# Quarter-width first V products, idle-time matmuls, and an earlier memory update in an attention and gMLP block

## The chip, the core and the metric

The kernel runs on one core of one Trainium2 chip. The core has five engines that each work through their own queue of instructions in order: TensorE (PE, with the loading of weights shown apart as PEld), VectorE (DVE), ScalarE (ACT), GpSimd (POOL) and SyncE (SP). In this kernel SP only issues transfers (DMA). The metric is the device time of one execution in microseconds (us), median of several runs. Before the change three runs took 826.48, 826.85 and 830.27 us.

## What is computed

A block of two parts on a sequence of 2048 tokens with 1024 channels, all in bf16. Part A is attention with a compressive memory: 32 heads of 32 channels, four segments of 512 tokens. Within a segment it is causal softmax attention; from one segment to the next a memory `M` (32 by 32 per head) and its normalizer `z` are carried. Part B is a gMLP. Both have a layer norm ahead and a residual.

```python
def _A_ref(x, wq, wk, wv, wo, beta):      # x is layernorm of the input
    q, k, v = heads(x @ wq), heads(x @ wk), heads(x @ wv)
    g = sigmoid(beta)
    M = 0; z = 0
    for s in range(4):
        qs, ks, vs = q[:, :, s], k[:, :, s], v[:, :, s]
        p = softmax(qs @ ks.T * scale + mask)
        a_dot = p @ vs
        pq = phi(qs)                      # t + 1 where t > 0, else exp(t)
        a_mem = (pq @ M) / (pq @ z + 1e-6)
        outs.append(g * a_mem + (1 - g) * a_dot)
        pk = phi(ks)
        M = M + pk.T @ vs
        z = z + sum(pk)
    return concat(outs) @ wo
def _B_ref(x, w_in, w_sp, b_sp, w_out):   # x is layernorm of h
    z = gelu(x @ w_in)
    z1, z2 = z[:, :1792], layernorm(z[:, 1792:])
    return (z1 * (w_sp @ z2 + b_sp)) @ w_out
h = x + A(layernorm(x)); out = h + B(layernorm(h))
```

## The kernel before

A small recorder collects the instructions of each engine in the order of the program text and puts a semaphore wait wherever one engine's instruction touches what another has written or read. So the order in the text is the order of every queue. Two rules matter here: for PSUM, the memory that TensorE writes to, the recorder counts whole banks of 512 fp32 columns, and any access to a bank by another engine has to be over before the next one begins; and all transfers are issued by SP, in order.

**Start.** SP issues the loads: x chunks 0 and 1 (`XCH`, 128 tokens each, 256 KB), the first 512 columns of `WV` (1 MB), x chunks 2 and 3, the first 256 columns of `WK` and of `WQ`, `beta`, and the rest of `WV`, `WK`, `WQ` and all of `WO` (9 MB in all). POOL and DVE build the identity matrix `IDENT`. For each of the four chunks of segment 0, DVE computes the layer norm statistics (`stats_of`), POOL the reciprocal root, DVE normalizes into `LNO` (`ln_apply`); TensorE transposes it in eight blocks and ACT evicts them to `XNT` (`pe_T`), and a V product follows (`proj_v`, eight matmuls accumulating over 1024 channels into one bank, evicted by ACT into `V`). Then `gates()` computes the gate `GS`, its complement `OMG` and the table `MASKG` (on DVE), with which the memory is masked by head; two products make K and Q of unit 0 (`proj_qk`), and `phi(0)` its feature maps.

**Units.** The loop from line 650 runs over 32 units n; unit n is segment s = n // 8 and a group c = n % 8 of four heads. In every unit TensorE does, in this order: logits of round 0; a filling f1 (K of the next unit); PV of round 2 of the unit before; logits of round 1; filling f2 (Q of the next unit); PV of round 0; logits of round 2 and, from segment 1 on, the product with the memory (`mem`); filling f3; PV of round 1; the memory update (`state`); filling f4 in segments 1 to 3. The logits go to banks 0 to 3, PV accumulates in banks 4 and 5, and everything else takes banks 6 and 7 in turn (`next_bank`). Fillings f3 and f4 are V products of 512 columns or output products (`wo`) of the segment before. Behind logits, ACT computes the exponentials (`E`) and POOL zeroes the masked triangle. `norm` (DVE) normalizes the output of a unit out of banks 4 and 5; the first PV of the next unit can start only after it. `mem_norm` (DVE: `rdm`, `tm`) does the same for the memory's part, behind ACT's third exponential.

`phi(n + 1)` is called behind f3: ACT's exp into `ETMP`, three DVE instructions, and SP's transposing transfer of the keys' features into `PK`. `state(n)` multiplies `PK` with `V` into a bank; DVE adds the bank to `MSUM` and writes the masked copy `MZB`, which `mem` of the next segment reads. It does nothing in segment 3.

In the units with c < 4 of segments 0 to 2, SP also loads an x chunk of the next segment. Its layer norm is done in three steps by `bg_pop`, called three times in a unit: statistics on DVE (first call), the root on POOL (second), normalization on DVE and a transposing transfer into `XNT` by SP (third). The chunk's load is issued at the head of its unit, behind the transfers that SP has in its queue from the unit before. Output rows (`HCH`) of `wo` take the same three steps.

**Behind the units** come the two gated halves of part B, the spatial product and the output product, long runs of 512-column matmuls on TensorE; the change doesn't touch them.

Of the kernel before, what the change touches and what calls it, by code (L numbers as in the profile page):

```python
# [8 lines left out]
ACTF = mybir.ActivationFunctionType  # L9
# [248 lines left out]
def bass_sequential_preLN__memory_aug_infini_attn__mixer_gmlp__prompt_kernel(  # L258
# [17 lines left out]
    pe, act, dve, pool, sp = R.pe, R.act, R.dve, R.pool, R.sp  # L276
# [6 lines left out]
    def tens(name, shape, dt, off):  # L283
        sz = int(np.prod(shape[1:])) * mybir.dt.size(dt)
        assert off % 32 == 0 and off + sz <= ARENA, (name, off, sz)
        t = nc.alloc_sbuf_tensor_at(name, list(shape), dt, offset=abase + off)
        R.space[t[:].tensor.name] = ("sbuf", off)
        return t
# [14 lines left out]
    IDENT = cb("ident", [128, 128], BF16)  # L303
# [9 lines left out]
    MHALF = cb("mhalf", [128, 1], F32)  # L313
# [4 lines left out]
    RDM = cb("rdm", [128, 4, 4], F32)  # L318
# [5 lines left out]
    WV = tens("wv", [128, 8, D], BF16, 46 * K)  # L324
# [12 lines left out]
    ETMP = b2("etmp", [128, 2, L], BF16)  # L337
# [4 lines left out]
    V = b2("v", [128, 4, H, 34], BF16)  # L342
# [17 lines left out]
    PS = nc.alloc_psum_tensor("ps", [128, 8, 512], F32)  # L360
    R.space[PS[:, 0, :].tensor.name] = ("psum", 0)

    def bank(b):
        return PS[:, b, :]
# [6 lines left out]
    def next_bank():  # L371
        b = rot["banks"][rot["n"] % len(rot["banks"])]
        rot["n"] += 1
        return b

    def mm8(dst, lhs, rhs, n=8):
        for i in range(n):
            pe.matmul(dst, lhs(i), rhs(i), start=(i == 0), stop=(i == n - 1))


    def x_load(tc):
        sp.dma_start(XCH[tc % 4][:], x2d[tc * 128:(tc + 1) * 128, :])

    def wcols(ap, lo, hi):
        return ap[:, lo:hi].rearrange("(c p) n -> p c n", p=128)

    x_load(0)
    x_load(1)
    sp.dma_start(WV[:, :, 0:512], wcols(A_wv, 0, 512))
    x_load(2)  # L390
    x_load(3)
    sp.dma_start(WK[:, :, 0:256], wcols(A_wk, 0, 256))
    sp.dma_start(WQ[:, :, 0:256], wcols(A_wq, 0, 256))
    sp.dma_start(BETAB[:], A_beta.partition_broadcast(128))
# [4 lines left out]


    pool.memset(MHALF[:], -0.5)
    pool.iota(IOT[:], [[1, 128]], base=0, channel_multiplier=-1)
    pool.memset(V[:, :, :, 32:34], 1.0)
    pool.memset(BLK[:], 1.0)
# [6 lines left out]
    def gates():  # L411
        act.activation(GS[:], BETAB[:], ACTF.Exp, scale=-1.0)
        dve.tensor_single_scalar(GS[:], GS[:], 1.0, ALU.add)
        dve.reciprocal(GS[:], GS[:])
        dve.tensor_scalar(OMG[:].rearrange("p c i -> p (c i)"), GS[:], -1.0, 1.0, ALU.mult, ALU.add)
        dve.tensor_copy(MASKG[:, :, :, 0:32],
                        GS[:].rearrange("p (c i) -> p c i", i=4).unsqueeze(3).to_broadcast([128, NQ, 4, 32]))
        for i in range(4):
            dve.tensor_single_scalar(MASKG[:, :, i, 0:32], MASKG[:, :, i, 0:32], BLK[:, i:i + 1], ALU.mult)
        for c in range(NQ):  # L420
            dve.tensor_copy(MASKG[:, c, :, 32], BLK[:])
# [33 lines left out]


    def proj_v(s, tcl, half):
        b = next_bank()
        xt = XNT[s % 2]
        mm8(bank(b), lambda i: xt[:, i, tcl * 128:(tcl + 1) * 128],  # L460
            lambda i: WV[:, i, half * 512:(half + 1) * 512])
        act.activation(V[:, tcl, half * 16:(half + 1) * 16, 0:32],
                       bank(b).rearrange("p (h d) -> p h d", d=32), ACTF.Copy)

    def proj_qk(n, which):
        s, c = divmod(n, NQ)
# [19 lines left out]
    def logits(n, rnd):  # L486
        qk = QK[n % 3]
        parts = {0: ((0, 0, 512),), 1: ((1, 0, 384), (3, 384, 128)), 2: ((2, 0, 256),)}[rnd]
        wid = (512, 512, 256)[rnd]
        e = E[rnd]  # L490
        for j, o, w in parts:
            for i in range(4):
                pe.matmul(PS[:, i, o:o + w], qk[32 * i:32 * (i + 1), 1, j * 128:(j + 1) * 128],
                          qk[32 * i:32 * (i + 1), 0, j * 128:512], start=True, stop=True,
                          tile_position=(32 * i, 0))
        if rnd == 2 and n >= NQ:
            mem(n)
        act.activation(e[:, :, 0:wid], PS[:, 0:4, 0:wid], ACTF.Exp, scale=float(SCALE))
        for j, o, w in parts:
            d = e[:, :, o:o + 128]  # L500
            pool.affine_select(out=d, in_=d, pattern=[[0, 4], [1, 128]], compare_op=ALU.is_ge, fill=0.0,
                               base=0, channel_multiplier=-1)
        if rnd == 2 and n >= NQ:
            mem_norm(n)
# [18 lines left out]
    def mem(n):  # L523
        c = n % NQ
        for cq in range(4):
            pe.matmul(PS[:, cq, 256:388], PQK[n % 3][:, 0, cq * 128:(cq + 1) * 128], MZB[:, c, :, 0:33],
                      start=True, stop=True)

    def mem_norm(n):
        om = PS[:, 0:4, 256:388].rearrange("p q (i d) -> p q i d", d=33)  # L530
        dve.tensor_single_scalar(RDM[:], om[:, :, :, 32], float(MEM_EPS), ALU.add)
        dve.reciprocal(RDM[:], RDM[:])
        dve.tensor_tensor(TM[:], om[:, :, :, 0:32], RDM[:].unsqueeze(3).to_broadcast([128, 4, 4, 32]), ALU.mult)
# [16 lines left out]
    def state(n):  # L550
        s, c = divmod(n, NQ)
        if s == NSEG - 1:
            return
        b = next_bank()
        for tcl in range(4):
            pe.matmul(PS[:, b, 0:132], PK[n % 3][:, tcl, :], V[:, tcl, 4 * c:4 * c + 4, 0:33],
                      start=(tcl == 0), stop=(tcl == 3))
        if s == 0:
            dve.tensor_copy(MSUM[:, c, :], PS[:, b, 0:132])
        else:  # L560
            dve.tensor_tensor(MSUM[:, c, :], MSUM[:, c, :], PS[:, b, 0:132], ALU.add)
        dve.tensor_tensor(MZB[:, c, :, 0:33], MSUM[:, c, :].rearrange("p (i d) -> p i d", d=33), MASKG[:, c, :, :],
                          ALU.mult)


    def xr_load(tc):
        sp.dma_start(XR[tc % 2][:], x2d[tc * 128:(tc + 1) * 128, :])
# [15 lines left out]
    def ln_tasks(src, dst, tcl):  # L583
        lnq[0].append((src, dst, tcl))
# [16 lines left out]
    def stats_of(tc):  # L601
        ks[tc] = ln_stats(XCH[tc])
        ln_rstd(ks[tc])

    stats_of(0)
    stats_of(1)
    for tc in range(4):
        o = ln_apply(XCH[tc], ks[tc])
        if tc < 2:
            stats_of(tc + 2)  # L610
        pe_T(XNT[0], tc, o)
        proj_v(0, tc, 0)
    gates()
    proj_qk(0, 1)
    proj_qk(0, 0)
# [34 lines left out]
    for n in range(LAST + 1):  # L650
        s, c = divmod(n, NQ)
        f1, f2, f3, f4 = [], [], [], []
        if n < LAST:
            f1, f2 = [("qk", n + 1, 1)], [("qk", n + 1, 0)]
        if s == 0:
            f3 = [("v", 0, c, 1)] if c < 4 else [("v", 1, c - 4, 0)]
        elif s < NSEG - 1:
            if c < 2:
                f3, f4 = [("v", s, 2 * c, 1)], [("v", s, 2 * c + 1, 1)]
            elif c < 6:  # L660
                f3, f4 = [("wo", s - 1, c - 2, 0)], [("wo", s - 1, c - 2, 1)]
            else:
                f3, f4 = [("v", s + 1, 2 * (c - 6), 0)], [("v", s + 1, 2 * (c - 6) + 1, 0)]
        else:
            if c < 4:
                f3 = [("v", s, c, 1)]
            if c in (2, 3):
                f4 = [("wo", s - 1, 0, c - 2)]
            elif c in (4, 5):
                f3 = [("wo", s - 1, 1, c - 4)]  # L670
            elif c == 6:
                f3, f4 = [("wo", s - 1, 2, 0)], [("wo", s - 1, 2, 1)]
            elif c == 7:
                f1, f2 = [("wo", s - 1, 3, 0)], [("wo", s - 1, 3, 1)]
                f3, f4 = [("z2", 0, 0)], [("z2", 0, 1)]

        def fill(lst):
            for u in lst:
                {"v": proj_v, "wo": wo, "qk": proj_qk, "z2": z2_group}[u[0]](*u[1:])

        if s < NSEG - 1 and c < 4:
            x_load(4 * (s + 1) + c)
            ln_tasks(XCH[c], XNT[(s + 1) % 2], c)
        if s > 0 and c == 1:
            xr_load(4 * (s - 1))

        logits(n, 0)
        fill(f1)
        if n > 0:
            pv(n - 1, 2)  # L690
        bg_pop()
        logits(n, 1)
        fill(f2)
        pv(n, 0)
        logits(n, 2)
        fill(f3)
        if n < LAST:
            phi(n + 1)
        pv(n, 1)
        bg_pop()  # L700
        state(n)
        fill(f4)
        bg_pop()
        if n in (28, 29):
            win_load(n - 28)
# [31 lines left out]
    for k in range(4, 8):  # L737
        lo, w = CH[k][1:]
        for fl in range(w // 128):
            fc = lo // 128 + fl  # L740
            for s in range(NSEG):
                b = next_bank()
# [11 lines left out]
    for tb in range(4):  # L754
# [4 lines left out]
        for fc in range(14):  # L759
            b = next_bank()  # L760
# [3 lines left out]
        for tcl in range(4):  # L764
            tc = 4 * tb + tcl
            fin = FIN[tc % 3]
            sp.dma_start(fin[:], out2d[tc * 128:(tc + 1) * 128, :])
            for half in range(2):
                b = next_bank()
# [34 lines left out]
```

The softmax here doesn't subtract the row's maximum and nothing guards it: scores larger than these inputs give would overflow.

## Time and profile before

| what | value |
|---|---|
| three runs | 826.48, 826.85, 830.27 us |
| the profiled execution | 827.13 us, its span 825.4 us |
| granted clock of TensorE | 1.00 |
| moved by DMA | 64.79 MB, 78 GB/s over the span |

Busy time by stage, us:

| stretch of the span | what runs | PE | DVE | ACT |
|---|---|---|---|---|
| 0 to 36 | start, unit 0 | 22.21 | 13.51 | 15.30 |
| 36 to 99 | units 1 to 7, segment 0 | 60.16 | 30.56 | 55.09 |
| 99 to 182 | segment 1 | 76.09 | 59.34 | 58.35 |
| 182 to 266 | segment 2 | 76.42 | 56.84 | 58.09 |
| 266 to 336 | segment 3 | 68.01 | 44.69 | 50.06 |
| 336 to 825 | part B | 484.33 | 163.67 | 64.95 |

The profile is one execution, with the start and length of every instruction. A row of a timeline has the start in us from the span's start, the length in us of the run of like instructions, the engine, the line, the operation, `out<-in`, the shape and the count; in brackets stands how long the engine was idle before and which event ended that. All rows name line 209, since the recorder issues every instruction there: the tile's name tells which one it is. Tiles have buffer numbers behind their names (`xch_92` is x chunk 0 of a segment, `pk_103` the first of three PK buffers). Stages are cut at round times, so a unit at an edge counts partly on both sides.

### The profile page before, as it was taken

What the parts mean: (1) busy time and instruction counts of PE and PEld (TensorE: products, weight loads), DVE (VectorE), ACT (ScalarE), POOL (GpSimd) and SP (SyncE); (2) the same over time, 40 slices, a digit from 0 to 9 for tenths busy, and PEclk for the clock granted to TensorE, in tenths of its full rate; (3) what the DMA queues carried; (4) which work ended last, traced back from release to release, by engine and by line L of the source; (5) the groups of instructions that cost most, each with busy time, mean ns of one, the idle gap of its engine ahead of it and who ended that gap; (6) DMA issues with size and microseconds to landing.
All of it is one profiled execution on the core that took longest, in us unless ns stands there. A gap on an engine that the chain in (4) does not pass through costs nothing.

```text
span 825.4 us, 12334 instructions
## 1 busy us (share of the span) xinstructions
PE 787.2 (95%) x5258; PEld 384.3 (47%) x5344; DVE 368.6 (45%) x753; ACT 301.8 (37%) x351; POOL 120.8 (15%) x234
## 2 busy tenths in 40 slices
PE   4899998998899999999999999999999999999998
PEld 2445444444444555455554444444444444444443
DVE  4454568756775568564456000043233314323432
ACT  2788866776667876133333333200000000000000
POOL 2143233323332233000033000000000000000000
PEclk9999999999999999999999999999999999999999
DMA  8631344344422224841013400190170035012002
GB/s 276 218 81 34 78 91 114 65 87 93 116 65 53 45 84 123 200 106 52 3 50 96 83 1 1 57 243 1 56 155 0 7 91 114 0 52 58 0 8 84
DMA packets 124808, 64.79 MB, mean 78 GB/s; under 512 B 94800, under 2 KB 113744, under 8 KB 124752
## 3 DMA queue, kind: packets, MB, share of 16 engines
q1 hardware_dynamic: 124752, 63.99, 31.2%
q8 instruction: 42, 0.69, 0.3%
q14 instruction: 14, 0.11, 0.1%
HBM read 32.51 MB, written 8.39 MB: 50 GB/s over the span
## 4 chain that ended last, share of the span: by engine, by line
PE 80%; DVE 9%; DMA 5%; ACT 3%; issue 2%; SPq 1%; POOL 0%
PE ps L209 80%; DMA xch_93<-in_A_x_dram 1%; DMA xch_95<-in_A_x_dram 1%; DMA xch_94<-in_A_x_dram 1%; DMA wv<-in_A_wv_dram 1%; ACT e_108 L209 1%; DVE stats_60 L209 1%; DVE stats_62 L209 1%; DVE rdm L209 1%; SPq L209 1%; ACT v L209 1%; DVE tm L209 1%; ACT etmp L209 1%; DVE etmp L209 1%; DVE stats_59 L209 1%
## 5 line engine op out<-in xcount | busy, mean ns | idle before, releaser
L209 PE MATMUL ps<-w_out,yT 128*128 128x512 bf16 x439 | 96.9, 379 | 0.5
L209 PE MATMUL ps<-wspT_119,z_117 128*128 128x512 bf16 x439 | 96.5, 379 | 0.5
L209 PE MATMUL ps<-wspT_120,z_117 128*128 128x512 bf16 x439 | 96.5, 379 | 0.5
L209 ACT ACTIVATE e_106<-ps 128x2048 bf16<-128x2048 f32 x32 | 60.0, 1874 | 36.2 <-PE ps L209 36.2
L209 PEld LDWEIGHTS ps<-wspT_119,z_117 128*128 128x128 bf16 x448 | 43.8, 98 | 52.8
L209 PEld LDWEIGHTS ps<-wspT_120,z_117 128*128 128x128 bf16 x448 | 43.8, 98 | 52.9
L209 PEld LDWEIGHTS ps<-w_out,yT 128*128 128x128 bf16 x448 | 43.8, 98 | 52.9
L209 PE MATMUL ps<-wo,oT 128*128 128x512 bf16 x243 | 57.2, 379 | 8.7 <-DVE hch_86 L209 3.0
L209 DVE TENSOR_TENSOR tmpg_126<-ps,brow_124 128x512 f32<-128x512 f32 x14 | 9.7, 690 | 117.6 <-DMA brow_124<-in_B_b_sp_dram 97.3
L209 ACT ACTIVATE z_117<-ps 128x448 bf16<-128x448 f32 x64 | 34.8, 544 | 74.7 <-PE ps L209 74.7
L209 ACT ACTIVATE e_107<-ps 128x2048 bf16<-128x2048 f32 x32 | 60.1, 1877 | 0.5 <-PE ps L209 0.5
L209 ACT ACTIVATE z1T<-ps 128x512 bf16<-128x512 f32 x56 | 33.4, 597 | 63.3 <-PE ps L209 63.3
L209 DVE BATCH_NORM_STATS2 zst<-z_117 128x6 f32<-128x448 bf16 x64 | 39.1, 620 | 32.6 <-ACT z_117 L209 32.6
L209 POOL TENSOR_SCALAR_AFFINE_SELECT e_107<-e_107 128x512 bf16<-128x512 bf16 x64 | 39.6, 643 | 46.9 <-ACT e_107 L209 46.9
L209 PEld LDWEIGHTS ps<-wo,oT 128*128 128x128 bf16 x256 | 23.6, 98 | 33.5 <-DVE hch_86 L209 3.3
L209 POOL TENSOR_SCALAR_AFFINE_SELECT e_106<-e_106 128x512 bf16<-128x512 bf16 x32 | 20.3, 634 | 126.9 <-ACT e_106 L209 126.9
L209 PE MATMUL ps<-wv,xnT_77 128*128 128x512 bf16 x121 | 30.5, 396 | 7.0 <-ACT xnT_77 L209 3.7
L209 ACT ACTIVATE e_108<-ps 128x1024 bf16<-128x1024 f32 x32 | 32.7, 1023 | 10.5 <-PE ps L209 10.3
L209 PE MATMUL ps<-xnT_78,wk 128*128 128x512 bf16 x125 | 29.7, 380 | 2.1 <-DVE msum L209 1.6
L209 ACT ACTIVATE v<-ps 128x512 bf16<-128x512 f32 x32 | 19.1, 597 | 34.4 <-PE ps L209 34.4
L209 PE MATMUL ps<-xnT_77,wk 128*128 128x512 bf16 x125 | 29.7, 380 | 2.0 <-DVE msum L209 1.3
L209 PE MATMUL ps<-xnT_77,wq 128*128 128x512 bf16 x120 | 28.8, 380 | 1.2 <-issue 0.8
(206 smaller groups left out, 1068.0 us busy)
## 6 DMA issues: line engine op xcount, KB each, us to landing
w_out<-in_B_w_out_dram SPq DMA_DIRECT2D x1, 3584.0 KB, 13.4
wv<-in_A_wv_dram SPq DMA_DIRECT2D x2, 1024.0 KB, 7.4
wo<-in_A_wo_dram SPq DMA_DIRECT2D x1, 2048.0 KB, 16.6
xr_83<-in_A_x_dram SPq DMA_DIRECT2D x8, 256.0 KB, 3.0
xr_84<-in_A_x_dram SPq DMA_DIRECT2D x8, 256.0 KB, 3.1
win_114<-in_B_w_in_dram SPq DMA_DIRECT2D x2, 896.0 KB, 5.5
wk<-in_A_wk_dram SPq DMA_DIRECT2D x1, 1536.0 KB, 10.0
wq<-in_A_wq_dram SPq DMA_DIRECT2D x1, 1536.0 KB, 12.8
```

What stands on the lines that cost most here:

```text
L209: ins = getattr(e, op.name)(*op.args, **op.kw)
```

## The change

It has four parts.

1. The load of the first 512 columns of WV is split into two of 256 columns; the second goes behind x chunks 2 and 3.
2. The V products of segment 0 that come ahead of the units are made in eight pieces of 256 columns (`proj_v_cols`) instead of four of 512, in an order written out in `late`: none behind the transposes of chunk 0, one behind chunk 1, one behind chunk 2, six behind chunk 3. So the transposes of a chunk come ahead of the product of the chunk before.
3. Ahead of the first transposes TensorE does 12 matmuls of `IDENT` with a zeroed `ETMP` into bank 7, whose result nobody reads; DVE zeroes `ETMP` first, and ACT does an Exp on one column of `MHALF`.
4. `state(n)` moves from behind PV of round 1 to behind logits of round 2, ahead of filling f3 and of `phi(n + 1)`; unit 0 keeps the old place. The part of `gates()` that fills `MASKG` becomes `mask_g()` and is called in unit 0 at that new place.

```diff
     x_load(0)
     x_load(1)
-    sp.dma_start(WV[:, :, 0:512], wcols(A_wv, 0, 512))
+    sp.dma_start(WV[:, :, 0:256], wcols(A_wv, 0, 256))
     x_load(2)
     x_load(3)
+    sp.dma_start(WV[:, :, 256:512], wcols(A_wv, 256, 512))
     sp.dma_start(WK[:, :, 0:256], wcols(A_wk, 0, 256))
...
     pool.memset(MHALF[:], -0.5)
+    dve.memset(ETMP[:], 0.0)
+    act.activation(RDM[:, 0, 0:1], MHALF[:], ACTF.Exp)
...
         dve.tensor_scalar(OMG[:].rearrange("p c i -> p (c i)"), GS[:], -1.0, 1.0, ALU.mult, ALU.add)
+
+    def mask_g():
         dve.tensor_copy(MASKG[:, :, :, 0:32],
                         GS[:].rearrange("p (c i) -> p c i", i=4).unsqueeze(3).to_broadcast([128, NQ, 4, 32]))
         for i in range(4):
...
     def proj_v(s, tcl, half):
+        proj_v_cols(s, tcl, half * 512, 512)
+
+    def proj_v_cols(s, tcl, lo, w):
         b = next_bank()
         xt = XNT[s % 2]
-        mm8(bank(b), lambda i: xt[:, i, tcl * 128:(tcl + 1) * 128],
-            lambda i: WV[:, i, half * 512:(half + 1) * 512])
-        act.activation(V[:, tcl, half * 16:(half + 1) * 16, 0:32],
-                       bank(b).rearrange("p (h d) -> p h d", d=32), ACTF.Copy)
+        mm8(PS[:, b, 0:w], lambda i: xt[:, i, tcl * 128:(tcl + 1) * 128], lambda i: WV[:, i, lo:lo + w])
+        act.activation(V[:, tcl, lo // 32:(lo + w) // 32, 0:32],
+                       PS[:, b, 0:w].rearrange("p (h d) -> p h d", d=32), ACTF.Copy)
...
+    for i in range(12):
+        pe.matmul(bank(7), IDENT[:], ETMP[:, 0, :], start=True, stop=True)
     stats_of(0)
     stats_of(1)
+    late = {1: [(0, 0)], 2: [(1, 0)], 3: [(2, 0), (0, 1), (1, 1), (3, 0), (2, 1), (3, 1)]}
     for tc in range(4):
...
         pe_T(XNT[0], tc, o)
-        proj_v(0, tc, 0)
+        for t_, q in late.get(tc, []):
+            proj_v_cols(0, t_, 256 * q, 256)
     gates()
...
         logits(n, 2)
+        if n == 0:
+            mask_g()
+        else:
+            state(n)
         fill(f3)
         if n < LAST:
             phi(n + 1)
         pv(n, 1)
         bg_pop()
-        state(n)
+        if n == 0:
+            state(n)
         fill(f4)
```

## The prediction

> **What bounds the kernel now.** I read the page's shares first, then the chain that ended last in order of time, then the timeline of its first 70 us and of one segment behind it, and the transfers.
>
> ```profile
> PE 787.2 (95%) x5258; PEld 384.3 (47%) x5344; DVE 368.6 (45%) x753; ACT 301.8 (37%) x351; POOL 120.8 (15%) x234
> ...
> PE 80%; DVE 9%; DMA 5%; ACT 3%; issue 2%; SPq 1%; POOL 0%
> ```
>
> TensorE is busy for 787.2 of 825.4 us, so all a reordering can touch is the 38 us in which it idles: 14 lie ahead of 36 us, 3 between 36 and 99, 15 between 99 and 266 (segments 1 and 2), 7 behind (the table by stage). The change edits the first three stretches. The start:
>
> ```profile
> 10.27 3.57 PE L209 MATMUL ps<-wv,xnT_77 128*128 128x512 bf16 x8 [2.26 <-DMA wv<-in_A_wv_dram]
> 10.82 1.42 DVE L209 BATCH_NORM_STATS2 stats_61<-xch_94 128x6 f32<-128x512 bf16 x2 [3.90 <-DMA xch_94<-in_A_x_dram]
> ...
> 14.89 3.36 SPq L209 DMA_DIRECT2D wo<-in_A_wo_dram  x1
> ...
> 15.65 0.55 DVE L209 TENSOR_SCALAR lno_88<-xch_95,mv_66,rs_70 128x1024 bf16<-128x1024 bf16 x1 [0.76 <-POOL rs_70 L209]
> 15.74 1.90 PE L209 MATMUL ps<-wv,xnT_77 128*128 128x512 bf16 x8 [1.12 <-ACT xnT_77 L209]
> ...
> 24.48 1.89 PE L209 MATMUL ps<-xnT_77,wk 128*128 128x512 bf16 x8
> ```
>
> The first V product takes 3.57 us, the next 1.90, for equal work: TensorE starts at half speed. It waits for WV (landed 10.13), then for each transposed chunk of x; the first K product starts at 24.48. The units' loop:
>
> ```profile
> 26.12 0.69 DVE L209 COPY maskg<-gs 128x1024 f32<-128x1024 f32 x1
> 26.84 1.52 DVE L209 TENSOR_SCALAR maskg<-maskg,blk 128x256 f32<-128x256 f32 x4
> 28.40 0.67 DVE L209 COPY maskg<-blk 128x4 f32<-128x4 f32 x8
> ...
> 30.07 2.08 SPq L209 DMA_TRANSPOSE pk_103<-pqk_99  x1
> 32.19 0.58 SPq L209 DMA_DIRECT2D xch_92<-in_A_x_dram  x1
> ...
> 35.05 1.42 DVE L209 BATCH_NORM_STATS2 stats_59<-xch_92 128x6 f32<-128x512 bf16 x2 [5.01 <-DMA xch_92<-in_A_x_dram]
> ...
> 40.41 0.58 SPq L209 DMA_DIRECT2D xch_93<-in_A_x_dram  x1
> ...
> 40.88 0.56 PE L209 MATMUL ps<-v,e_106 128*128 128x33 bf16 x16
> ```
>
> ```profile
> 40.41 3.41 DMA xch_93<-in_A_x_dram
> ...
> 48.94 2.99 DMA xch_94<-in_A_x_dram
> ...
> 57.05 2.85 DMA xch_95<-in_A_x_dram
> ...
> 64.87 3.59 PE ps L209 x52
> ```
>
> To be seen: DVE idles 5.01 us before stats_59, and from there to 64.87 the chain is a ring: x chunk load, its statistics on DVE, phi, SP's two transposes, the next load, 8.1 to 8.5 us a turn, where units without a load take 7.65 (first PV at 72.54, then 80.19). So TensorE in segment 0 follows when those chunks land, not when it began.
>
> **The front.** SP's loads share one queue. 1.05 MB of WV stand ahead of x chunk 2 now, half of it after. The transfers' rate is 356 GB/s at 5 to 8 us (WV, rows of 1 KB) and 324 at 8 to 11 (WK, WQ, rows of 512 B): 2.95 us for the 512 columns of WV, 1.62 for 256 of them (0.52 MB). So chunk 2 lands 1.3 us earlier, 9.5, and DVE's statistics and normalizations after it too: the last one ends at 16.2 - 1.3 = 14.9. The chunk's eight transposes (0.61) end by 15.5 at latest, 15.0 if the wait for POOL shrinks; its eviction (1.02) at 16.1. Six V products remain then. A product of 256 columns has no row; half of the 1.73 between the starts of the 512-column products at 24.48 and 26.21 is 0.86 (if weight loads set it, eight transposes' 0.61 is below that, and the full 1.73 above). Six take 5.2, K starts at 20.2: 4.3 earlier. WK, landed at 13.1, is late by less than 1.
>
> The idle-time matmuls: 12 at about 0.43 (spacing of the weight loads at 10.65 and 11.08) are 5.2 us from 1.7 to 6.9, where the first transposes wait for lno_88 until 6.98; they cost nothing, and a spill of 0.5 would vanish in the wait for chunk 2. The memset of ETMP comes before IDENT on DVE: between 0.32 (POOL's memset of V) and 0.55 (lno_88, as many elements), hidden since stats_59 starts at 3.32. The dummy Exp (0.22, as gs) lies in ACT's idle time to 8.05. The Trainium skill, "TensorE: Matmul & The Clock Gate", section on the HAM clock gate, says that after an idle window of about 3.4 us the clock halves again, which speaks against the idle-time matmuls: between the first transposes (7.6) and the second ones (11) TensorE idles about that long. By the row K starts at 20.2, by the rule up to 1 us later. "DMA: Bandwidth & Descriptors", Specifications, gives line rate from 512 B up; the rows' 324 against 356 say there is a tenth to lose, and by the rule chunk 2 would land 0.15 sooner.
>
> **Where the 4.3 us go.** phi(0) ends at 30.04 - 4.3 = 25.7, SP issues pk_103, then the load of chunk 4 at about 28.0. But the weight stream is no earlier: WO lands at 14.89 + 16.6 = 31.5, and with WV in 512 B rows (+0.3, and up to +0.7 by the 300 GB/s around 10.5) at about 32.0. Chunk 4 queues behind it and pk_103: 32.0 + 0.6 (pk's data, 31.4 to 32.0) + 0.7 (the distance between the landings of chunks 2 and 3) = 33.3. Bounds: 28.0 + 2.86, as the load of 32.19 took, = 30.9; and, if SP's transpose is held until WO is down (its 2.08 ended 0.65 after 31.5; others take 1.2), 32.0 + 0.65 + 0.04 + 2.86 = 35.6. I take 33.3, nearest to the order of the queue.
>
> Behind stats_59 in DVE's queue now stands mask_g, which ran before phi(0) until now: 2.85 (26.12 to 28.97), with phi(1), msum, mzb, the normalization and norm(0) behind it; TensorE waits for msum (a bank for unit 1's Q) and for norm(0) (unit 1's first PV), SP for phi(1) and the normalization. Against before, at the PV of 64.87:
> - landing: 33.3 - 35.05 = -1.75
> - mask_g: +2.85
> - phi(1) no longer waits for ACT's exp (36.63 to 37.78 is 1.15, its work 0.85): -0.3
> - memory update ahead of phi in units 1 and 2: SP's transpose of PK is issued 0.22 + 0.30 (msum, mzb) later, the next transpose and load are queued behind it, measured back to back (46.34, 47.65, 48.94): +0.45 a turn, two turns, +0.9.
>
> Sum +1.7; by the bounds of the landing -0.7 and +4.0. If mask_g stood in DVE's hole before 33.3, the sum were -1.15.
>
> **The memory update in segments 1 and 2.** It takes bank 6 or 7 in the rotation before the third filling, so the fourth filling now waits for its msum, and the next K for the third filling's eviction.
>
> ```profile
> 110.23 0.69 DVE L209 TENSOR_TENSOR tm<-ps,rdm 128x512 f32<-128x512 f32 x1
> ...
> 112.58 1.90 PE L209 MATMUL ps<-xnT_78,wk 128*128 128x512 bf16 x8 [0.54 <-DVE msum L209]
> ...
> 121.30 1.67 PE L209 MATMUL ps<-wo,oT 128*128 128x512 bf16 x7 [1.15 <-DVE hch_85 L209]
> ```
>
> K waits for an msum that stands behind phi; the second output product waits for the first one's hch (0.69) behind tm. After: msum (0.21) stands directly behind tm. Eight units with output products: 0.69 - 0.21 less 0.1, -0.4 each, -3.2. Three units with V fillings and early chunks (14, 15, 22): K's wait of 0.4 to 0.86 goes, but ACT's e_106 behind the V eviction is the next to end, -0.4 each, -1.2. Units 8, 9 and 17, whose chunk lands late: the fourth filling waits for tm + msum, 100.53 + 0.21 against its 99.67, +1.1, less K's 0.7 gone, +0.4 each, +1.2. Five turns of load, phi, transposes (units 8 to 11, 17 to 19): +0.45, +2.2. Together -1.0; bounds -4.4 (no costs) and +3.4 (no gains). Segment 3 has no update, and everything behind only shifts.
>
> **Sum.** 1.7 - 1.0 = +0.7 on the profiled 827.13 (span 825.4 and 1.7 around it) is 827.8; that execution was 0.28 above the median of 826.85, so 827.6.
>
> **The rivals.**
> - *The front's gain lasts* (faster). Chunk 4 lands at 30.9, as its own 2.86 says, and the update's costs don't show: -0.7 - 4.4 = -5.1, 821.8. For it: ring turns of 8.1 leave TensorE only 0.5 over 7.65, and the waits on msum and hch are in the trace. Against: DMA moves 370 to 390 GB/s without a hole from 16 to 30 us, so nothing queued at 26 can pass.
> - *SP holds chunk 4 back* (slower). The transpose of PK stays in SP's queue until WO is down, chunk 4 lands at 35.6: +4.0; with the update's own sum at nought, 830.9, at its upper bound 834.3. Decides from a landing of 35.7 on. For it: that first transpose took 2.08. Against: it may be the busy queue alone.
> - *The clock doesn't stay up* (the change doesn't do what it says): a V product of 256 columns at the first one's pace is 1.8 (half of 3.57) for 0.95, K starts near 21. Chunk 4 still comes behind WO, so the end stays 827.6; it belongs to the forecast.
>
> **How the numbers follow.** Three runs spread over 3.8 us, so 0.5% (4.1 us) is what can be told from no change: under 822.7 is faster, over 831.0 slower. The forecast (within) gets 0.57; the first rival, with milder mixes of its two halves that still pass 4.1, 0.20; the second with the update's costs 0.23. The range: the front's bounds with the update's -1.0 give 825.2 to 829.9 (-0.7 - 1.0 and +4.0 - 1.0 on 826.85); the update's ends reach 3 to 4 further, but both at their ends are unlikely: 822.6 to 832.0.
>
> **What would show it.** K's first product near 20.2; the first V product of 256 columns near 0.95, not 1.8; statistics of chunk 2 at 9.5. Then stats_59 for chunk 4 near 33.3, mask_g directly behind it, a hole of some 3 us on TensorE before unit 1's Q released by msum, its first PV at 41 like before, and the fifth PV near 66.6. In segments 1 and 2 fourth fillings that wait for msum, and no K that does. It is wrong if stats_59 starts before 31.5 or after 35, if TensorE keeps more than 2 us of its lead at the fifth PV, or if segments 1 and 2 change by more than 3 us.

## The result, and the profile after

The changed kernel took 836.3 us (median of four runs, 834.16 to 839.31) beside 826.66 us for the kernel before (825.64 to 830.27): 1.0111 of it, with an interval of 1.0065 to 1.0157. It is slower by 9.6 us, above the predicted 827.6 and outside the predicted range of 822.6 to 832.0. The profiled execution was the slowest of the four (839.31 us, span 837.6).

The page's shares and the chain that ended last, after:

```profile
PE 796.3 (95%) x5302; PEld 392.2 (47%) x5388; DVE 372.5 (44%) x754; ACT 302.8 (36%) x356; POOL 121.7 (15%) x234
...
PE 77%; DVE 10%; DMA 6%; ACT 4%; issue 2%; SPq 1%
```

TensorE is busy 9 us longer, though the change gives it only some 5 us of idle-time matmuls (5.17 in the timeline) in a stretch where it had nothing to do. So part of its own products became slower. The span grew by 12.2 us in all, so the waits ahead of TensorE grew too: DVE's share of the chain went from 9 to 10%, DMA's from 5 to 6. The start, from the timeline of the first 26 us:

```profile
8.39 1.42 DVE L209 BATCH_NORM_STATS2 stats_61<-xch_94 128x6 f32<-128x512 bf16 x2 [1.28 <-DMA xch_94<-in_A_x_dram]
...
10.52 1.03 PE L209 MATMUL ps<-ident,lno_89 128*128 128x128 bf16 x8 [2.74 <-DVE lno_89 L209]
...
11.34 1.91 PE L209 MATMUL ps<-wv,xnT_77 128*128 128x256 bf16 x8
...
13.64 1.04 PE L209 MATMUL ps<-wv,xnT_77 128*128 128x256 bf16 x8
...
20.42 1.67 PE L209 MATMUL ps<-xnT_77,wk 128*128 128x512 bf16 x7
```

K starts at 20.42 instead of 24.48. The idle-time matmuls did not keep the clock up: the first transposes, right behind them, take 0.62, but after 2.74 us without work the second ones take 1.03, and the first quarter product 1.91, the second 1.04. The timeline of 26 to 50 us:

```profile
27.11 0.57 SPq L209 DMA_DIRECT2D xch_92<-in_A_x_dram  x1
...
33.31 1.42 DVE L209 BATCH_NORM_STATS2 stats_59<-xch_92 128x6 f32<-128x512 bf16 x2 [7.55 <-DMA xch_92<-in_A_x_dram]
...
34.89 0.64 DVE L209 COPY maskg<-gs 128x1024 f32<-128x1024 f32 x1
...
35.57 1.91 DVE L209 TENSOR_SCALAR maskg<-maskg,blk 128x256 f32<-128x256 f32 x4
...
37.52 1.14 DVE L209 COPY maskg<-blk 128x4 f32<-128x4 f32 x8
...
39.74 0.28 DVE L209 COPY msum<-ps 128x132 f32<-128x132 f32 x1
...
40.30 2.85 PE L209 MATMUL ps<-xnT_77,wq 128*128 128x512 bf16 x7 [4.41 <-DVE msum L209]
...
42.95 0.66 PE L209 MATMUL ps<-v,e_106 128*128 128x33 bf16 x16
...
45.50 1.42 DVE L209 BATCH_NORM_STATS2 stats_60<-xch_93 128x6 f32<-128x512 bf16 x2 [3.59 <-DMA xch_93<-in_A_x_dram]
...
47.09 0.24 DVE L209 COPY msum<-ps 128x132 f32<-128x132 f32 x1
...
47.61 1.67 PE L209 MATMUL ps<-xnT_77,wk 128*128 128x512 bf16 x7 [0.81 <-DVE msum L209]
```

Read from the top: chunk 4, issued at 27.11 behind the weights, lands for stats_59 at 33.31; DVE then fills MASKG until 38.56; msum comes behind it; TensorE has waited 4.41 us for msum's bank, and its Q then takes 2.85 us instead of 1.67. Unit 1's first PV starts at 42.95, 2.07 later than before. In the next unit msum stands behind the statistics of a late chunk, and K waits 0.81 for it. Over the whole execution this line of the waits (us in total, times, longest) went from the first row, before, to the second, after:

```profile
PE ps L209 <- DVE msum L209: 2.9, 5, 0.8
...
PE ps L209 <- DVE msum L209: 22.0, 20, 4.4
```

Where each stage ended, as the start of a unit's first logits, in us and against before (the first column is the kernel before):

| unit | before | after | e1_front | e2_state | e11_all_x_state |
|---|---|---|---|---|---|
| 0 | 28.79 | -4.28 | -4.21 | -0.13 | -5.30 |
| 1 | 36.41 | -3.29 | -3.13 | -0.13 | -3.94 |
| 2 | 44.06 | +2.34 | -2.47 | -0.14 | -3.26 |
| 5 | 68.07 | +4.21 | -0.23 | +2.26 | -3.61 |
| 8 | 91.02 | +5.63 | -0.23 | +2.97 | -2.35 |
| 11 | 122.91 | +6.19 | -0.64 | +3.21 | -2.42 |
| 12 | 133.85 | +10.21 | +1.71 | +3.73 | -3.43 |
| 19 | 206.26 | +10.82 | +2.27 | +3.17 | -5.51 |
| 20 | 217.96 | +12.74 | +4.22 | +3.25 | -7.28 |
| 24 | 258.85 | +12.19 | +4.22 | +2.44 | -8.07 |

Each column is one profiled execution: that of after is the slowest of its four, that of e1_front lies 1.6 us above its median, that of e2_state 3.0 below. The table shows three places of loss after: unit 1 (5.6 us), units 2 to 7 (3.3), and, among smaller ones, two single units, 11 and 19 (4.0 and 1.9). Units 8 and 17 lost 1.5 and 1.9 too, but 10 and 18 gave 1.1 and 1.5 back. From unit 24 on everything is only shifted. Unit 11, from the timeline of 120 to 150 us of after, and behind it the same unit before (124 to 137):

```profile
132.76 1.93 SPq L209 DMA_DIRECT2D xch_95<-in_A_x_dram  x1
...
137.56 1.42 DVE L209 BATCH_NORM_STATS2 stats_59<-xch_95 128x6 f32<-128x512 bf16 x2 [3.61 <-DMA xch_95<-in_A_x_dram]
...
140.93 3.19 PE L209 MATMUL ps<-wo,oT 128*128 128x512 bf16 x7 [3.91 <-DVE msum L209]
...
144.60 2.80 PE L209 MATMUL ps<-xnT_78,wk 128*128 128x512 bf16 x8
```

```profile
125.63 0.58 SPq L209 DMA_DIRECT2D xch_95<-in_A_x_dram  x1
...
128.65 1.42 DVE L209 BATCH_NORM_STATS2 stats_59<-xch_95 128x6 f32<-128x512 bf16 x2 [1.14 <-DMA xch_95<-in_A_x_dram]
...
132.02 1.90 PE L209 MATMUL ps<-wo,oT 128*128 128x512 bf16 x8 [1.18 <-DVE hch_86 L209]
```

The segment's last chunk lands 4.80 us after its issue began instead of 3.02, and 1.35 of these 1.78 us lie in SP's issue itself (1.93 for 0.58). TensorE's second output product waits 3.91 instead of 1.18, and after that wait it and the next K run at about half speed (3.19 for seven matmuls that take 1.67; 2.80 for 1.90). The granted clock says the same, in two of the rows cut by time (columns: stretch, length, busy time of PE, PEld, DVE, ACT, POOL with counts, granted clock, DMA share, GB/s):

```profile
40.00:50.00 10.00, 8.88 (x84) 4.69 (x87) 5.59 (x17) 5.18 (x7) 2.22 (x4) 0.83 0.34 71
...
130.00:150.00 20.00, 15.93 (x141) 7.68 (x140) 13.74 (x31) 10.75 (x10) 5.56 (x12) 0.83 0.60 119
```

Before, both stretches stand at 1.00.

### The profile page after: what moved, and what is told of

The parts are those of the page before. It is cut to its first block, busy times and chain, and to the rows that moved or that the text cites. A ratio compares the mean times of both kernels' runs of the same rounds, so it can differ in the third digit from the quotient of the medians.

```text
span 837.6 us, 12417 instructions
## 1 busy us (share of the span) xinstructions
PE 796.3 (95%) x5302; PEld 392.2 (47%) x5388; DVE 372.5 (44%) x754; ACT 302.8 (36%) x356; POOL 121.7 (15%) x234
## 3 DMA queue, kind: packets, MB, share of 16 engines
HBM read 32.51 MB, written 8.39 MB: 49 GB/s over the span
## 4 chain that ended last, share of the span: by engine, by line
PE 77%; DVE 10%; DMA 6%; ACT 4%; issue 2%; SPq 1%
PE ps L209 77%; DMA xch_94<-in_A_x_dram 2%; DVE tm L209 2%; ACT e_108 L209 2%; DMA xch_95<-in_A_x_dram 1%; SPq L209 1%; ACT e_106 L209 1%; DMA xch_92<-in_A_x_dram 1%; DMA xch_93<-in_A_x_dram 1%; DVE stats_61 L209 1%; DVE rdm L209 1%; DVE stats_59 L209 1%; DMA pk_104<-pqk_100 1%; DVE stats_60 L209 1%; ACT v L209 0%
## 5 line engine op out<-in xcount | busy, mean ns | idle before, releaser
L209 PE MATMUL ps<-wo,oT 128*128 128x512 bf16 x242 | 59.6, 392 | 9.2 <-DVE msum L209 8.5
L209 DVE BATCH_NORM_STATS2 zst<-z_117 128x6 f32<-128x448 bf16 x64 | 39.1, 620 | 32.5 <-ACT z_117 L209 32.5
L209 PE MATMUL ps<-xnT_77,wk 128*128 128x512 bf16 x124 | 29.8, 382 | 3.6 <-DVE msum L209 3.4
L209 PE MATMUL ps<-wv,xnT_77 128*128 128x512 bf16 (+1 forms) x154 | 29.8, 343 | 3.3 <-DVE msum L209 3.0
L209 ACT ACTIVATE v<-ps 128x512 bf16<-128x512 f32 (+1 forms) x36 | 19.8, 550 | 33.4 <-PE ps L209 33.4
L209 PE MATMUL ps<-wv,xnT_78 128*128 128x512 bf16 x120 | 28.5, 379 | 3.0 <-DVE msum L209 2.7
```

Source lines behind the costliest of these rows:

```text
L209: ins = getattr(e, op.name)(*op.args, **op.kw)
```

## The experiments

Runs of one group were made on one chip beside the kernel before (828.74, 828.92, 828.58 and 827.88 us in the four groups), and each time is given with its ratio to that and the interval.

**The parts alone.** e1_front is the changed kernel with the update and the MASKG fill back at their old places:

```diff
     gates()
+    mask_g()
...
         logits(n, 2)
-        if n == 0:
-            mask_g()
-        else:
-            state(n)
         fill(f3)
...
-        if n == 0:
-            state(n)
+        state(n)
```

> Only the start is changed (WV in two loads, V in quarters, idle matmuls, memset, Exp); MASKG is filled in the old place and the memory update stays in its old place. Theory of waits: the start's lead of 4.3 us shrinks to the earlier landing of x chunk 4 (33.3 for 35.05, and 0.3 that phi(1) no longer waits), so some 2 us less than before: 824 to 825.5. Rival, the start itself loses (rows of 512 B, a clock that falls back in the gap behind the idle matmuls): 828 or more.

829.69 us, 1.0009 [0.9992, 1.0027]: no gain. In its profiled execution (831.32) the 4.2 us at the start were there, were gone by unit 8 (-0.23), and units 11 and 19 turned them into a loss of 4.22. So the front doesn't lose only to chunk 4, but also far behind it.

e2_state is the kernel before with the update alone moved:

```diff
         logits(n, 2)
+        if n > 0:
+            state(n)
         fill(f3)
...
         bg_pop()
-        state(n)
+        if n == 0:
+            state(n)
```

> Only the memory update is moved (units 1 and later); start and MASKG as before. Theory of waits: the fourth filling's and K's waits for msum behind late statistics, and the halved clock after them, cost by themselves: between units 2 and 24 the changed kernel lost 9.9 us, so 833 to 837. Rival, the move is neutral as forecast and the table's new place is the loss: 825 to 828.

833.21 us, 1.0053 [1.0036, 1.0069]: in the theory's range. Its reasons show only in part: the profiled execution was its fastest (830.19), and there all of the loss up to unit 24 lies in segment 0 (+2.97 at unit 8), segments 1 and 2 give 0.5 back, and no product behind a wait in the units runs at half speed.

e3_front_mask is e1_front with `mask_g()` at the change's place (`if n == 0: mask_g()` ahead of f3).

> The start and the table's new place, the memory update in its old place. Theory of waits: the table stands 3.7 us behind the statistics of chunk 4 and unit 1 loses 5.6 of the lead of 4.3, then the units run as before: 827 to 830. Rival, the table is the main loss: 833 or more.

833.41 us, 1.0057 [1.0038, 1.0077]: the rival. Unit 1 took 12.80 us, against 7.65 before and 13.28 after, so the MASKG fill makes the hole in unit 1 without the update's move.

e5_mask_early is the changed kernel with `mask_g()` directly behind `phi(0)`, where DVE waits for chunk 4 anyway.

> The changed kernel with the table filled right behind phi(0), where DVE idles until chunk 4 lands; the update moved. Theory of waits: unit 1 keeps its length of 7.65 plus at most 1, so 4 to 5 us are saved against the changed kernel's 836.3: 831 to 833. Rival, the table is the main loss: 827 or less. If the start is the loss: no change, 836.

835.04 us, 1.0066 [1.0044, 1.0088]. Unit 1 fell from 13.28 to 8.31 us, but half of it was lost at once in unit 2 (10.86, 8.25 after), and units 11 and 19 took 14.20 and 14.33. By the ratios it saves 0.0045, 3.7 us.

g3_front_state is the missing corner: the changed kernel with `mask_g()` behind `gates()`, at its old place.

> The new front and the memory update's new place, MASKG filled at its old place. If the parts' costs add up (front +1.0, update +4.4): 833 to 835, and MASKG's place is worth 2 to 3.5 of the whole. Rival (they don't add, because the update's extra work on DVE only hurts behind the MASKG fill): 829 to 831.

832.54 us, 1.0059 [1.0038, 1.0079]. The ratios add up: 0.0009 for the front and 0.0053 for the update make 0.0062, and with 0.0048 for MASKG's place (e3_front_mask less e1_front) the whole is 0.0110, where 0.0111 was measured. In us of 827: +0.7, +4.4, +4.0. The intervals leave a doubt of 1.5 us for the front and the update, of 2 for MASKG's place and of 4 for the whole.

**Why units 11 and 19 lose.** In five profiles that start earlier (after, e1_front, e3_front_mask, e5_mask_early, g3_front_state) the last chunk of segments 1 and 2 landed 3.61 to 4.80 us after its issue, for 3.02 and 3.19 before; in e6_act_evict and e7_keep_busy it did not (2.92 to 3.47). Unit 11 of e1_front, from its timeline:

```profile
125.00 0.58 SPq L209 DMA_DIRECT2D xch<-in_A_x_dram  x1
...
129.10 1.42 DVE L209 BATCH_NORM_STATS2 stats<-xch 128x6 f32<-128x512 bf16 x2 [2.23 <-DMA xch<-in_A_x_dram]
...
132.47 3.15 PE L209 MATMUL ps<-wo,oT 128*128 128x512 bf16 x8 [2.27 <-DVE hch L209]
```

The landing is 1.08 us later than before (4.10 for 3.02), the wait 1.09 longer, and behind it the product runs at about half speed: 3.15 for 1.90. 1.09 + 1.25 = 2.34 is the unit's growth, 10.94 to 13.29. What else was on the way between 125 and 130 us is in the transfers of e1_front (the strips have 40 slices of 0.125 us; the rows below are queue, kind, packets, MB, share of 16 engines):

```profile
GB/s 189 211 213 215 215 203 205 209 193 138 15 133 0 0 0 33 115 213 180 426 360 426 360 410 393 393 311 246 180 49 16 33 16 33 0 0 0 0 0 0
...
q8 instruction: 1, 0.02, 1.6%
```

Behind the burst of the loads, from 128.6 to 129.3, a trickle of 16 to 33 GB/s is left, as if one or two of the 16 DMA engines were still busy, and one transfer of TensorE's instructions (0.69 MB in 42 packets in all, so 16 KB each) lies in the stretch. Twelve profiled kernels issue the chunk loads of units 1 to 19 at the old place and have no other data ahead of them, eleven loads in each, 132 in all. In 23 such an instruction transfer began between 0.4 us ahead of the issue and 0.5 us ahead of the statistics: they landed in 2.90 to 4.80 us, mean 3.85, and 17 of them above 3.5. The other 109 took 2.78 to 3.46, mean 3.05. The moment decides: in all 17 the transfer began between 0.2 us ahead of the issue and 2.1 us behind it, in the six that were in time at 2.4 us or later. Where it began within 0.2 us of the issue, SP's issue itself took 1.26 to 1.93 us in six of seven loads (at most 0.59 in the 109). Where these transfers fall depends on how many instructions TensorE has done, and the change puts 88 more (matmuls and weight loads) into the start. Three runs shift them on purpose. f1_fetch_before is the kernel before with 44 small matmuls more:

```diff
+    for i in range(44):
+        pe.matmul(PS[:, 7, 0:64], IDENT[:], IDENT[:, 0:64], start=True, stop=True)
     stats_of(0)
```

> The kernel before with 44 narrow matmuls (64 columns, bank 7, nobody reads it) ahead of the first transposes: 88 more instructions on TensorE (a weight load and a matmul each), as many as the changed start adds, in its idle time. Theory of the instruction fetch: the 16 KB transfers that fetch TensorE's instructions then fall 88 instructions earlier in the loop and meet the load of x chunk 3 in units 11 and 19, whose landing takes 4.1 us or more for 3.0 to 3.2, and those units grow from 10.9 and 11.7 to 13 or more: 2 to 5 us slower than before. Rival, the late landing in the runs with the changed start comes from the DMAs of the start (one more, 512 B rows): no change, within 1 us of before.

832.38 us, 1.0038 [1.002, 1.0056]. The first logits start 2.0 us later, so part of the loss may be the matmuls' own time; but four chunks landed in 3.95, 4.05, 4.33 and 4.23 us, the last two in units 11 and 19, which took 12.26 and 14.67 us instead of 10.94 and 11.70. The profiled execution (835.57) is the slowest of its ten. f2_fetch_front is e1_front with 96 idle-time matmuls of 64 columns for the 12 of 512, so with 168 more instructions:

> The changed start alone (as e1_front), with 96 idle matmuls of 64 columns for the 12 of 512: TensorE's instruction count is then 256 above before, one whole 16 KB fetch, so fetches fall where they fell before. Theory of the instruction fetch: units 11 and 19 are back at 11 and 11.8, and the start's 2 us show: 1.5 to 3 us faster than before. Rival: units 11 and 19 stay above 13, no faster than before.

827.29 us, 0.9995 [0.9979, 1.0011]. No load of segments 1 and 2 had an instruction transfer in it (chunk 5 of segment 0 had one, 3.93), and unit 11 took 11.13; unit 19 still took 12.96, since behind its wait of 2.09 us (1.94 before) the clock was down, though the chunk landed in 3.34. Unit 11 and both landings bear the theory out, unit 19 and the time don't: the gain on e1_front (0.0014) is within the intervals. g1_after_phase makes the same exchange in the changed kernel:

> The changed kernel with 96 idle-time matmuls of 64 columns in place of 12 of 512: about the same TensorE time, 168 more TensorE instructions, so its instruction transfers fall at other places. Theory (units 11 and 19 lose because such a transfer falls into the load of the segment's last chunk): 1 to 4 us below the changed kernel's 836.4, and units 11 and 19 shorter than 13 us together with landings near 3.1. Rival (they lose to the memory update and to the earlier start themselves): within 1 us of 836.4.

833.75 us, 1.0071 [1.0049, 1.0092], 0.0040 (3.3 us) below the changed kernel by the ratios, whose intervals overlap. Unit 11:

```profile
132.60 0.58 SPq L209 DMA_DIRECT2D xch<-in_A_x_dram  x1
...
135.81 1.42 DVE L209 BATCH_NORM_STATS2 stats<-xch 128x6 f32<-128x512 bf16 x2 [2.02 <-DMA xch<-in_A_x_dram]
...
139.00 1.67 PE L209 MATMUL ps<-wo,oT 128*128 128x512 bf16 x7 [2.15 <-DVE msum L209]
```

The issue is at almost the same time as after (132.76), the landing takes 3.21 for 4.80, the wait is 2.15 for 3.91, and the product runs at full speed: the unit took 11.67 us for 14.96.

g2_row and g2c_rows16 should have shown the delay by itself, with 16 KB of data ahead of chunks 5 to 7 of the kernel before, as one row and as 16 rows:

```diff
+            if s == 0 and c > 0:
+                sp.dma_start(ROW[0:1, :], x2d[0:8, :].rearrange("(o r) d -> o (r d)", o=1))
             x_load(4 * (s + 1) + c)
```

> The kernel before, with one row of 16 KB, into one partition, loaded on SP's queue directly ahead of each of x chunks 5, 6 and 7. Theory (a transfer of 16 KB that holds one of the 16 DMA engines for about 1 us delays a load's landing by as much): the three chunks land 3.9 to 4.3 us after their issue in place of 2.9 to 3.4, and units 2 to 4 grow by 0.5 to 1.5 each. Rival (the landing depends on the whole of the bytes or on SP): 2.9 to 3.4.

> The control of g2_row: the same 16 KB as 16 rows of 1 KB, into 16 partitions. Theory: landings of 2.9 to 3.4, as without it. Rival: as late as in g2_row.

Chunks landed in 3.26, 2.74 and 2.79 us with the row and in 4.42, 2.85 and 2.69 with its control. The row delays nothing, though it was on its way together with the chunk: it moved from 42.26, 51.15 and 59.96 us for 1.02, 0.86 and 0.66, and the chunks' own first packets began at 42.68, 51.48 and 59.82. So 16 KB on one engine beside a load are not enough to make it late. The one late landing is in the control, and an instruction transfer fell into it. (One time each: 831.54 and 829.05 us.) That an instruction transfer makes a load late rests on the 132 loads and on the landings in the three runs that shift them; it was not produced by itself, and how it does it stays open.

**The hole in unit 1.** e7_keep_busy gives TensorE work in the wait, to tell the halved clock from the wait:

```diff
         logits(n, 1)
+        if n == 1:
+            for i in range(18):
+                pe.matmul(bank(6), IDENT[:], WV[:, 0, 0:512], start=True, stop=True)
         fill(f2)
```

> The changed kernel with 18 matmuls into bank 6 (free then, nobody reads them) in the hole that unit 1 has ahead of its Q product. Theory of the halved clock: Q's eight matmuls run at 0.21 each again (1.7 to 1.9 us for 2.85) and unit 1 is 12.0 to 12.4 long for 13.28, some 1.2 us less than the changed kernel's +9.6. Rival, the slow Q is not the clock after idling: Q stays at 2.85, unit 1 at 13.3.

836.57 us, 1.0108 [1.0071, 1.0145]. The clock stayed up (Q 1.90 us, unit 1 12.02), but behind the next wait, 1.87 us for msum in unit 2, it was down (K 3.58, unit 2 11.20 for 8.25): nothing was won. e6_act_evict lets ACT copy the update's bank out, so that its bank is free before DVE comes to msum:

```diff
+        act.activation(STMP[:], PS[:, b, 0:132], ACTF.Copy)
         if s == 0:
-            dve.tensor_copy(MSUM[:, c, :], PS[:, b, 0:132])
+            dve.tensor_copy(MSUM[:, c, :], STMP[:])
         else:
-            dve.tensor_tensor(MSUM[:, c, :], MSUM[:, c, :], PS[:, b, 0:132], ALU.add)
+            dve.tensor_tensor(MSUM[:, c, :], MSUM[:, c, :], STMP[:], ALU.add)
```

> The changed kernel, with the memory update's bank copied out by ACT into a temporary tile, so that TensorE's fourth filling waits for ACT and no longer for msum behind mask_g, statistics and phi on DVE. Theory (in unit 1 Q waits for msum because mask_g stands ahead of it on DVE; 3 of its 4.4 us of wait and the halved clock behind it are due to that): unit 1's Q starts at 37 to 38 in place of 40.3 and takes 1.7 to 1.9, and the time falls by 2 to 4 us, to 832 to 834. Rival (unit 1 is held by its PV, which waits for norm(0) behind the same mask_g): Q starts early, but the first PV of unit 1 stays at 42.5 to 43 and the time within 1.5 us of 836.5.

830.89 us, 1.0033 [1.0013, 1.0054], more than either theory said, and for another reason. Unit 1 is as the rival had it, from its timeline:

```profile
37.05 1.67 PE L209 MATMUL ps<-xnT,wq 128*128 128x512 bf16 x7 [0.16 <-issue]
42.40 0.56 PE L209 MATMUL ps<-v,e 128*128 128x33 bf16 x16 [3.67 <-DVE otok L209]
...
43.37 2.93 PE L209 MATMUL ps<-wv,xnT 128*128 128x512 bf16 x8
```

Q is early, and PV then waits 3.67 us for the normalization (otok) behind the same MASKG fill; unit 1 took 12.76 us. The gain is in segments 1 and 2, where the fourth filling no longer waits for msum: unit 8 10.28 us for 11.74, units 13 to 17 9.67 to 9.90 for 9.93 to 11.89, and unit 11, with a landing of 3.08, 12.40 for 14.96. How much of it is the landing can't be told from one profile. Units 12 and 20 lost part of the gain again (12.20 each for 11.03 and 10.38).

**Taking the lap away.** What the losses behind unit 1 share, most of them, is that a chunk is asked for in the unit that needs it. e8_x_early asks one unit earlier, in the changed kernel:

```diff
     phi(0)
+    x_load(4)
...
         if s < NSEG - 1 and c < 4:
-            x_load(4 * (s + 1) + c)
+            if c == 0 and s > 0:
+                x_load(4 * (s + 1))
+            if c < 3:
+                x_load(4 * (s + 1) + c + 1)
```

> The changed kernel with each x chunk of the next segment loaded one unit earlier (the first of segment 0 stays). Theory of waits: the memory update costs because msum stands on DVE behind statistics that wait for a late chunk; with chunks in place units 2 to 4, 8 to 12 and 17 to 20 lose their excess (some 8 us of the 12 of the profile), unit 1 keeps it: 0 to 3 us slower than before. Rival, the update's place itself costs whatever the chunks do: 7 us slower or more.

824.62 us, 0.9952 [0.9937, 0.9968]: not slower, but faster than the kernel before, by 4.3 us, though unit 1 still took 14.14. The next three put this under the kernel before, under the front, and under all parts. b1_before_x:

> The kernel before, with nothing of the change, and each x chunk of the next segment loaded one unit earlier (chunk 4 directly behind phi(0)). Theory (in the units that load a chunk the lap of load, statistics, phi and transposes is longer than the unit's own work, whoever starts earlier): units 8 to 11, 18 and 19 fall from 10.3 to 11.7 us to about 10.0, units 2 to 4 to 7.65, together some 7 us: 820 to 823 against 828.8 for the kernel before. Rival (the earlier loads help the changed kernel alone, because only its chunks land late): 827 to 829.

821.93 us, 0.9924 [0.9905, 0.9942]. e10_all_x has the front, MASKG behind `phi(0)` and the update at its old place:

> The new front, MASKG filled behind phi(0), the memory update at its old place, x chunks one unit earlier. Theory (the front's 4 us were lost to late landings of chunks in units 2 or 3, 11 and 19, and to nothing else): it keeps 2 to 4 us of the front, 2 to 4 below b1_before_x, 817 to 820. Rival (what holds the early units back is chunk 4 behind the weights, or DVE's queue behind it, so the front is worth nothing whatever comes later): within 1 us of b1_before_x.

819.66 us, 0.9893 [0.9875, 0.9911]: 2.3 us of the front stay. Its timeline in unit 1:

```profile
28.35 1.78 DVE L209 TENSOR_SCALAR maskg<-maskg,blk 128x256 f32<-128x256 f32 x4
...
34.29 1.42 DVE L209 BATCH_NORM_STATS2 stats<-xch 128x6 f32<-128x512 bf16 x2 [3.46 <-DMA xch<-in_A_x_dram]
...
37.27 1.67 PE L209 MATMUL ps<-xnT,wq 128*128 128x512 bf16 x7 [0.37 <-DVE msum L209]
...
39.25 0.57 PE L209 MATMUL ps<-v,e 128*128 128x33 bf16 x16 [0.31 <-DVE otok L209]
```

MASKG lies in the hole ahead of chunk 4, DVE still idles 3.46 us, and Q waits 0.37 us instead of 4.41. e11_all_x_state adds the update's new place:

> As e10_all_x, but with the memory update at its new place: all three parts of the change with MASKG filled behind phi(0) and the chunks one unit earlier. Theory (the memory update's place costs DVE time ahead of phi in every unit of segment 0, 0.24 us in each of units 4 to 7 and more where the lap is tight, and gains little in segments 1 and 2): 1 to 3 us above e10_all_x. Rival (its cost was late landings only, and its waits saved in segments 1 and 2 show once the chunks are there): 1 to 4 us below e10_all_x. Against e8_x_early (824.6) it is 1.5 to 3.5 faster, the place of MASKG.

819.1 us, 0.9887 [0.9869, 0.9905], 0.6 below e10_all_x: neither theory, and less than the intervals can tell. With chunks that are there in time the update's place, on balance, costs nothing and gains about nothing. Against e8_x_early (0.9952) MASKG's place is worth 0.0065, 5.4 us. e11_all_x_state beats both kernels, by 9.5 us the one before.

## Why the prediction was wrong, step by step

- **The front was right up to unit 0.** K at 20.42 (20.2 predicted), chunk 2's statistics at 8.39 (9.5 predicted; 7.4 to 9.2 in other profiled runs). The clock did not stay up, as one of its rivals had it: 1.91 for the first quarter product where 0.95 stood in the forecast and 1.8 in the rival. That K came so near 20.2 all the same is partly luck: in the nine other profiled runs with this start it came between 19.40 and 22.38, at 20.3 or earlier where the clock was down for 3.4 us and at 21.4 or later where it was down for 6.8 (0.50 from 9.7 to 16.4 us in e10_all_x). The section on the HAM clock gate in the Trainium skill, "TensorE: Matmul & The Clock Gate", which it weighed, names an idle window of about 3.4 us; here 2.74 us were enough.
- **Chunk 4 was right.** 33.31, as worked out from the queue behind WO (33.3); 32.5 to 33.8 in the six other profiled runs that have this start and issue it at the same place. The rivals of 30.9 and 35.6 both fell.
- **MASKG's place was mis-sized.** 2.85 us were put in from the fill's own rows before; it took 3.67 (34.89 to 38.56), since one of its products and one of its copies were held up beside POOL's masking (0.75 us for 0.35, 0.64 for 0.17), and Q behind the wait ran at half speed, 2.85 for 1.67. First PV of unit 1: 42.95, not 41. The place costs 4.0 us by e3_front_mask less e1_front. The page before had the hole to put it in: DVE idles 5.01 us just ahead of stats_59.
- **The update in segment 0 was mis-sized.** +0.45 a turn in two turns was the SP delay alone. In e2_state the loss by unit 4 is +1.37, near that, but units 4 to 7 add 1.6 more. One reason is in the rows of after: msum's bank is taken before the third filling now, and msum stands in DVE's queue behind the statistics of a chunk that lands late, so that K waits (0.81 us at 47.61; 1.21 at 63.06, in unit 4 of e2_state). The prediction wrote this wait down for units 8, 9 and 17 and not for units 2 to 4. The other: units 5 to 7, without chunks to load, take 7.89 for 7.65, for in the new order the logits of round 1 wait 0.23 us for ACT's exponential. In all, the fifth unit's PV came at 69.10, not 66.6.
- **The step that failed: segments 1 and 2 as a small sum, and everything else behind as a shift.** The prediction took -1.0 there, with bounds of -4.4 and +3.4 from the update's waits alone. The update's own sum came near in the profile of e2_state (-0.5), but not its terms: units 8 and 17 lost 1.2 and 1.5 us where +0.4 stood, units 10 and 18 gained 1.2 and 1.3, so the sum is partly luck. But after, these segments lost 6.6 us (+5.63 at unit 8, +12.19 at unit 24), more than the 3 us that the prediction itself named as its sign of being wrong, and e1_front, without the update, lost 4.5 there. Of the 11.5 us by which the profile missed the forecast, 7.6 lie here and 3.9 in segment 0. The shift moves which chunk load an instruction transfer falls into; a landing 1.1 us later lengthens TensorE's wait by as much; behind the longer wait the clock is often down; and one or two products at half speed cost as much again. The update makes the same wait longer still, since msum comes behind the late statistics (3.91 us in unit 11 after, 2.27 in e1_front).
- **The range missed** since every term was counted as time that adds up. A wait on TensorE has a second price here, and that was seen in the start alone.
- **Open.** Executions of one kernel can differ by 5 us (e2_state 830.19 to 835.41), and one profile shows one of them; how often each load is late in the runs that were only timed isn't known. That the update costs 4.4 us by the medians and 2.4 up to unit 24 in its profiled execution is explained by late landings in the others only by argument.

## What to carry to other kernels

Follow a ring of load, statistics and products to where it closes: a lead at the start is worth what the loads later in the ring let through, and moving the loads one unit ahead was worth more (6.6 us on the unchanged kernel) than any part of the change. An instruction moved in a full in-order queue belongs in a hole that the profile shows, and every bank taken earlier makes its release a new wait, behind whatever stands ahead of the releasing instruction. Where TensorE's waits grow beyond the some 1.7 us from which its clock was seen to fall here, price them twice.

## What was not expected of the hardware

- **Instruction transfers meet loads.** TensorE's instructions come in 42 transfers of 16 KB. A 256 KB load that one of them falls into landed in 3.85 us in the mean instead of 3.05 (23 of 132 loads). It matters when: a transfer that began up to 2.1 us behind the issue made the load late, one at 2.4 us or later did not. Their place shifts with the number of instructions: with 44 small matmuls more at the start of the kernel before, late landings came into units 11 and 19 and the time grew by 0.0038 (part of it may be the matmuls' own), and with 84 more in the changed kernel both were gone, 0.0040 by ratios whose intervals overlap.
- **The clock falls after shorter waits than 3.4 us, and not at a fixed length.** In all 18 profiles, from 20 us to the end of the units, TensorE's waits of 1.3 to 1.68 us (18 of them) never brought the granted clock down, those from 2.88 us on (12) always did, and of the 21 between, from 1.69 to 2.73 us, 11 did. It went to 0.5, and for 3.4 or 6.8 us. The next two rows are from the timelines of e5_mask_early and f1_fetch_before: behind a wait of 1.69 us eight products take 3.08 us for 1.90, behind one of 2.73 seven run at full speed.

```profile
43.49 3.08 PE L209 MATMUL ps<-xnT,wk 128*128 128x512 bf16 x8 [1.69 <-DVE msum L209]
...
136.66 1.67 PE L209 MATMUL ps<-wo,oT 128*128 128x512 bf16 x7 [2.73 <-DVE hch L209]
```

The same section of the Trainium skill says that the window runs freely, so that the cost varies from run to run; that agrees with these rows.

- **DVE was held up beside POOL, one instruction at a time.** The MASKG fill's four products took 1.52 us at 26.84 before, where POOL was idle from 20 to 30, and 1.91 at 35.57 after, while POOL worked; the eight copies 0.67 and 1.14. All of it lies in one product (0.75 us for 0.35) and one copy (0.64 for 0.17), which ran beside POOL's masking of the exponentials; the two products beside POOL's one-column instructions took 0.35 as before.
